# One bank of a gated product moved from VectorE to ScalarE and GpSimd in every second block

## The chip, the cores and the metric

The kernel runs on one core of a Trainium2 chip. The metric is the device time of one launch in microseconds, from the first to the last instruction, with what the launch adds around it. One core has five engines that run side by side, each working through its own instructions in order: TensorE (PE in the profile; matmul), VectorE (DVE), ScalarE (ACT), GpSimd (POOL) and SyncE (SP), which here issues DMA transfers. Matmuls write to PSUM, which has 8 banks of 512 f32 values in each of 128 partitions; here GpSimd's instructions read and write SBUF only.

## The reference, cut to what matters

The input x is 4 batches of 12416 tokens with 128 channels. Two attention stages over 32 inducing vectors come first, then a gated feed-forward layer on all 49664 tokens:

```python
h = mab(I, x)              # 32 vectors look at all tokens of a batch (stage one)
y = mab(x, h)              # all tokens look at the 32 results (stage two)
gate = 1 / (1 + exp(-(y @ w_gate)))      # 128 -> 1536
val = y @ w_val                          # 128 -> 1536
out = (gate * val) @ w_out               # 1536 -> 128
```

`mab(q, kv)` is softmax(q kv^T / sqrt(128)) kv.

## The kernel before, in words

The result of stage two is never formed. Its softmax weights (32 per token) are multiplied with h w_gate and h w_val, which are small, so a hidden matmul has only 32 rows to contract. The gate is computed as 0.5 (1 + tanh(z / 2)); the 0.5 is applied at the end.

**Blocks and slots.** The tokens are worked in 97 *blocks*: 96 of 512 tokens (24 for each batch) and one of the four left-over chunks. The 1536 hidden units of a block are 12 chunks of 128 (j = 0 to 11). They are taken in *steps* that alternate between two chunks (two PSUM banks) and one chunk (one bank): 8 steps a block. Two steps are a *slot*: four slots a block, 388 in all, 96 a batch. Slots are counted from 0, within the kernel or, where said, within a batch.

**One step** has these parts. `product(t)` (L713) does the hidden matmuls of v (`hidden_mm`, L688) and then VectorE's product u = (t + 1) v (L717), which reads tanh's output t from SBUF and v from PSUM. `gate(t+2)` (L706) does the hidden matmuls of g and ScalarE's tanh (L711) two steps ahead. Each of v's and g's two-bank and one-bank tiles exists once, so v of step t + 2 can start when the product of step t has been read out, and g of step t + 2 when the tanh of step t has. Together with the output accumulator (`acc`) and one bank for side work (`m`) that is all eight banks.

**Projection.** After each odd step `project` (L725) takes chunks from a list in the order of j, up to three in a usual slot, and adds u times w_out into `acc`, four matmuls a chunk (L733). Behind the last chunk of a block ScalarE scales the block's output (L745) and SyncE stores it. That happens in the first slot of the next block.

**Side work** is what prepares later blocks: stage two of a group of 16 chunks (four blocks), stage one of the next batch, and the combining of stage one's sums. These are Python generators. `beside(slot)` (L819) runs once a slot, after the even step's product and gate: it starts what is due, issues DMA loads of x (from GpSimd) and transposes (from SyncE), and advances every active generator by one piece (`advance`, L794). A bare `yield` ends the slot's piece; "take" and "give" hold and free bank `m`, one holder at a time. All order is fixed when the program is written, and each engine then runs its instructions in that order, as soon as their inputs are there. The pieces that matter below:

- `stage2` (L468), 20 slots ahead of its group: scores on TensorE in two halves, VectorE's maximum and GpSimd's split of it into "hi" and "lo" (L371), their two matmuls onto the scores and ScalarE's exp (L384), the sums on GpSimd (L398), GpSimd's inverse by pow (L424), the normalised weights spread four times (`s2_spread`, L447, 128x2048 on GpSimd), and a transposing DMA from SyncE (L457). The last "group" of a batch is a single chunk.
- `stage1` (L248): scores and VectorE's maximum, ScalarE's exp with its sum, a transpose by DMA, six slots later 16 matmuls and a ScalarE copy.
- `combine` (L303): small copies on GpSimd (quad, L310), four VectorE minima, ScalarE's weights w1 (L322), GpSimd's products and an adding tree over the seven groups' sums (L325 to L333, called the tree below), then matmuls that give h and h w of the next batch.

Of the kernel before, what the change touches and what calls it, by code (L numbers as in the profile page):

```python
# [9 lines left out]
F32 = mybir.dt.float32  # L10
F16 = mybir.dt.float16
BF16 = mybir.dt.bfloat16
AF = mybir.ActivationFunctionType
ALU = mybir.AluOpType
AX = mybir.AxisListType

P = 128
GC = 16
# [9 lines left out]
def kernel(  # L28
# [9 lines left out]
    nc = tc.nc  # L38
    B, N, C = x.shape
    m = inducing.shape[0]  # L40
    F = moe_w_gate.shape[1]
    NJ = F // P
# [14 lines left out]
    bp = ctx.enter_context(tc.tile_pool(name="bp", bufs=2))  # L57
    s1p = ctx.enter_context(tc.tile_pool(name="s1p", bufs=4))
    s2p = ctx.enter_context(tc.tile_pool(name="s2p", bufs=2))
    up = ctx.enter_context(tc.tile_pool(name="up", bufs=6))  # L60
    tp = ctx.enter_context(tc.tile_pool(name="tp", bufs=4))
    op = ctx.enter_context(tc.tile_pool(name="op", bufs=4))

# [23 lines left out]
    def x_transpose_dma(b, s):  # L89
# [16 lines left out]
        out=identf[:],  # L106
        in_=identf[:],
# [140 lines left out]
    def stage1(b, s):  # L248
        yield "take"
        s1 = s1_score(b, s, "m")  # L250
        yield
        yield
        a1T = s1_exp(b, s, s1)
        yield "give"
        yield
        if groups[s][1] == GC:
            a1 = s1_turn_dma(b, s, a1T)
            for _ in range(S1_LAG):
                yield
            yield "take"  # L260
        else:
            yield "take"
            a1 = s1_turn_copy(s, s1_turn_pe(b, s, a1T))
            yield
        s1_sum(b, s, a1, "m")
        yield "give"


    hT16 = {}
# [33 lines left out]
    def combine(b):  # L303
        q = b % 2
        nm1, l1, hst = nm1s[q], l1s[q], hsts[q]
        while summed[b] < NS:
            yield
        quad = bp.tile([m, 4, NS], F32, tag="quad")
        for g in range(4):
            nc.gpsimd.tensor_copy(out=quad[:, g, :], in_=nm1[32 * g : 32 * g + 32, :])  # L310
        for _ in range(COMBINE_LAG):
            yield
        col = bp.tile([P, 1], F32, tag="col")
        for g in range(4):
            nc.vector.tensor_reduce(
                out=col[32 * g : 32 * g + 32, :],
                in_=quad[:].rearrange("k g s -> k (g s)"),
                axis=AX.X,
                op=ALU.min,
            )  # L320
        w1 = bp.tile([P, NS], F32, tag="w1")
        nc.scalar.activation(out=w1[:], in_=nm1[:], func=AF.Exp, bias=col[:], scale=-1.0)  # L322
        yield
        lw = bp.tile([P, NS], F32, tag="lw")
        nc.gpsimd.tensor_tensor(out=lw[:], in0=l1[:], in1=w1[:], op=ALU.mult)  # L325
        add_tree(lw, NS)
        e32l = bp.tile([P, m], F32, tag="e32l")
        nc.gpsimd.tensor_scalar_mul(out=e32l[:], in0=e32[:], scalar1=lw[:, 0:1])
        hx = bp.tile([P, NS, C], F32, tag="hx", bufs=1)
        nc.gpsimd.tensor_tensor(  # L330
            out=hx[:], in0=hst[:], in1=w1[:].unsqueeze(2).to_broadcast((P, NS, C)), op=ALU.mult
        )
        add_tree(hx, NS)  # L333
        for _ in range(COMBINE_LAG):
            yield
        yield "take"
        l_ps = ps.tile([P, m], F32, tag="m", name="l_ps")
        nc.tensor.matmul(l_ps[:], ones[:], e32l[:], start=True, stop=True)
        li = l_inverse(l_ps[:])
        yield "give"  # L340
        yield "take"
        h_ps = ps.tile([P, m], F32, tag="m", name="h_ps")
        nc.tensor.matmul(h_ps[:], hx[:, 0, :], e32[:], start=True, stop=True)
        h_take(b, h_ps[:], li)
        yield "give"
        yield


        hwt = bp.tile([P, NI, P], F16, tag="hw", bufs=B)
        for hf in range(2):  # L350
            yield "take"
            hw_ps = hw_fill(b, hf, "m")
            nc.scalar.copy(out=hwt[:, ts(hf, NI // 2), :], in_=hw_ps[:])
            yield "give"
        hw[b] = hwt
# [88 lines left out]
        )  # L444
        return rs[:, 0:n]

    def s2_spread(n, e, rs, eng):  # L447
        a2n = s2p.tile([P, GC, 4, m], F16, tag="a2n")
        eng.tensor_tensor(  # L449
            out=a2n[:, 0:n, :, :],  # L450
            in0=e.unsqueeze(2).to_broadcast((P, n, 4, m)),
            in1=rs.unsqueeze(2).unsqueeze(3).to_broadcast((P, n, 4, m)),
            op=ALU.mult,
        )
        return a2n
# [10 lines left out]
            a2[(b, c + j)] = (a2r, j)  # L466

    def stage2(b, c, n, soon=False):  # L468
        yield "take"
        s2 = ps.tile([P, GC, m], F32, tag="m", name="s2_ps")  # L470
        half = (n + 1) // 2
        s2_score(b, c, 0, half, s2)
        yield
        s2_score(b, c, half, n, s2)
        hi, lo = s2_max(n, s2)
        yield
        yield
        e = s2_exp(n, s2, hi, lo)
        yield "give"
        sme = s2_sum_pool(n, e)  # L480
        yield
        yield
        rs = (s2_inverse if soon else s2_inverse_pool)(n, sme)
        a2n = s2_spread(n, e[:, 0:n, :], rs, nc.gpsimd)
        yield
        yield
        s2_turn_dma(b, c, n, a2n, "a2r" if n == GC else "a2l")
# [15 lines left out]
    for p in range(-2, NS - 3):  # L503
# [11 lines left out]
        if p + 1 == EARLY - 1:  # L515
# [3 lines left out]
                out=nml[:, 0:1], in_=nm1[:, 0:EARLY], axis=AX.X, op=ALU.min  # L519
# [27 lines left out]
    c0, n = groups[sc]  # L547
# [17 lines left out]
    for g in range(4):  # L565
        nc.gpsimd.tensor_copy(out=quad[:, g : g + 1], in_=ml[32 * g : 32 * g + 32, :])
    nc.gpsimd.tensor_scalar(
        out=quad[:, 0:1],
# [105 lines left out]
    steps = []  # L674
# [6 lines left out]
    blocks.append([(b, 0, NLO) for b in range(B)])  # L681
    for i in range(len(blocks)):
        for j in range(0, NJ, 3):
            steps.append(dict(block=i, j0=j, cnt=2))
            steps.append(dict(block=i, j0=j + 2, cnt=1))
    NST = len(steps)

    def hidden_mm(st, what):  # L688
# [24 lines left out]
    def product(t):  # L713
        st = steps[t]
        hidden_mm(st, "v")
        st["u"] = up.tile([P, st["cnt"], 512], F16, tag=f"u{st['cnt']}", name="u16")
        nc.vector.scalar_tensor_tensor(  # L717
            out=st["u"][:], in0=st["t"][:], scalar=1.0, in1=st["v"][:], op0=ALU.add, op1=ALU.mult
        )

    acc = [None]
    queue = [(t, k) for t in range(NST) for k in range(steps[t]["cnt"])]
    queue.reverse()

    def project(upto, now, room):  # L725
        while queue and queue[-1][0] < upto and room > 0:
            t, k = queue.pop()
            st = steps[t]
            j = st["j0"] + k
            if j == 0:  # L730
                acc[0] = ps.tile([P, BC, C], F32, tag="acc", name="acc_ps")
            for i in range(BC):
                nc.tensor.matmul(  # L733
                    acc[0][:, i, :],
                    st["u"][:, k, ts(i, P)],
                    wo16[:, j, :],
                    start=(j == 0 and i == 0),
                    stop=(j == NJ - 1),
                    skip_group_check=True,
                )  # L740
            room -= 1
            if j == NJ - 1:
                block = blocks[st["block"]]
                o32 = op.tile([P, BC, C], F32, tag="o32")
                nc.scalar.mul(out=o32[:], in_=acc[0][:], mul=0.5)  # L745
                if len(block) == 1:
                    b, c, nb = block[0]
                    nc.sync.dma_start(ov[b, :, c : c + nb, :], o32[:])
                else:
                    nc.sync.dma_start(ov0[:, 0, :, :], o32[:])  # L750
                if now < NST:
                    return
# [38 lines left out]
    def taken():  # L791
        return holder[0] is not None or slot_now[0] < free_at[0]

    def advance(gen):  # L794

        if gen["ask"]:
            if taken():
                return
            holder[0] = gen
            gen["ask"] = False  # L800
        while True:
            try:
                said = next(gen["it"])
            except StopIteration:
                active.remove(gen)
                return
            if said == "take":
                if taken():
                    gen["ask"] = True
                    return  # L810
                holder[0] = gen
            elif said == "give":
                holder[0] = None
                free_at[0] = slot_now[0] + 1
                return
            else:
                return

    def beside(slot):  # L819
        slot_now[0] = slot  # L820
        while loads and loads[0][0] <= slot:
            _, what, b, g = loads.pop(0)
            if what == "x":
                x_load(b, g)
            else:
                x_transpose_dma(b, g)
        while work and work[0][0] <= slot:
            _, first, make = work.pop(0)
            active.append(dict(it=make(), ask=False, first=first))
        for gen in sorted(active, key=lambda e: e["first"]):  # L830
            advance(gen)

# [48 lines left out]
```

## Time and profile before

| | |
|---|---|
| median of 3 runs | 768.11 us (766.72 to 768.52) |
| the profiled execution's own time | 768.34 us |
| its span, first to last instruction | 766.5 us |
| mean granted TensorE clock | 0.989 |
| L717, VectorE's products, two banks | 388, mean 1220 ns |
| L717, VectorE's products, one bank | 388, mean 679 ns |
| L711, tanh, two banks and one bank | 388 each, mean 1030 and 606 ns |
| L745, block outputs on ScalarE | 97, mean 606 ns |
| L449, spread on GpSimd, 128x2048 | 23, mean 3610 ns |
| L427, pow of the inverse on GpSimd, 128x16 | 22, mean 2936 ns |

A line of the timeline gives the start in us, the time until the merged instructions end, the engine, the line of the kernel, the operation, output and inputs, and how many instructions are merged; in brackets stands how long the engine idled before and who released it. Instructions of one engine overlap a little (the next one starts before the last has written its end), so the distance between two starts is less than a duration; where that distance matters it is taken from the starts. A hidden step's time from start to start of the two-bank products is called the slot's length.

### The profile page before, as it was taken

Reading aid. Unit: us, or ns where it says so; the run is one execution under the profiler, and the core shown is the slowest. Engines: PE = TensorE matmul, PEld = TensorE weight load, DVE = VectorE, ACT = ScalarE, POOL = GpSimd, SP = SyncE. Lnnn points to the kernel's source line nnn. Section 1 sums busy time; section 2 is a strip of 40 time slices with the busy share of each in tenths; the row PEclk is TensorE's granted clock in tenths of the full one; section 3 lists DMA queues with packets and bytes.
Section 4 is the critical chain, followed back from the end, with each engine's and each line's share of the span. In section 5 each row is a group of like instructions: output and inputs, shape, how many; then the busy total and the mean of one; then the engine's idle time right before and its main releaser. Section 6 shows DMA issues by size and latency. Waiting matters only on the chain.

```text
span 766.5 us, 20798 instructions
## 1 busy us (share of the span) xinstructions
PE 669.1 (87%) x8167; PEld 402.6 (53%) x8167; DVE 736.3 (96%) x911; ACT 672.4 (88%) x1008; POOL 275.7 (36%) x439
## 2 busy tenths in 40 slices
PE   6788889889888888989888888888998888888887
PEld 4445555555555455555555545555555555555554
DVE  4889999999999999999999999999999999999997
ACT  4689889899898989989998989989999989889896
POOL 3535050582350441545513504147335135135100
PEclk9689999999999999999999999999999999999999
DMA  8979752604249525244138342121221121231211
GB/s 168 154 144 181 149 83 84 112 29 98 71 92 178 115 63 112 57 97 86 49 78 158 88 89 63 49 57 36 78 57 49 52 68 41 58 69 34 67 43 43
DMA packets 117730, 65.16 MB, mean 85 GB/s; under 512 B 101344, under 2 KB 102016, under 8 KB 117632
## 3 DMA queue, kind: packets, MB, share of 16 engines
q1 hardware_dynamic: 112192, 49.94, 27.9%
q0 software_dynamic: 5440, 13.90, 11.1%
q8 instruction: 64, 1.05, 0.6%
q14 instruction: 34, 0.28, 0.1%
HBM read 27.80 MB, written 25.43 MB: 69 GB/s over the span
## 4 chain that ended last, share of the span: by engine, by line
DVE 34%; PE 28%; issue 20%; ACT 14%; POOL 4%; DMA 1%; ACTq 0%; DVEq 0%; POOLq 0%
DVE u L717 30%; PE acc_ps L733 11%; PE v_ps L696 11%; ACT t L711 10%; PE s_ps L362 2%; DVE nm L190 2%; DVE nmx L373 2%; ACT a1T L203 1%; PE g_ps L696 1%; ACT e L395 1%; ACT o L745 1%; PE xt_ps L494 1%; POOL near L427 1%; PE s_ps L386 1%; DMA xn<-in_x_dram 1%
## 5 line engine op out<-in xcount | busy, mean ns | idle before, releaser
L717 DVE SCALAR_TENSOR_TENSOR u<-t,v_ps 128x1024 f16<-128x1024 f16 (+1 forms) x776 | 692.2, 950 | 11.3 <-ACT t L711 3.4
L711 ACT ACTIVATE t<-g_ps 128x1024 f16<-128x1024 f32 (+1 forms) x776 | 598.2, 818 | 68.2 <-PE g_ps L696 53.8
L696 PE MATMUL v_ps<-a2r,hwt 32*128 32x512 f16 (+1 forms) x1188 | 292.8, 371 | 79.3 <-DVE u L717 76.3
L733 PE MATMUL acc_ps<-wo,u 128*128 128x128 f16 x4656 | 328.6, 220 | 1.1
L733 PEld LDWEIGHTS <-u 128*128 128x128 f16 x4656 | 262.7, 98 | 97.4 <-issue 95.6
L696 PE MATMUL g_ps<-a2r,hwt 32*128 32x512 f16 (+1 forms) x1188 | 296.1, 378 | 0.3
L696 PEld LDWEIGHTS <-hwt 32*128 32x128 f16 x2400 | 100.0, 91 | 214.6 <-issue 168.7
L377 POOL CAST hi<-nmx 128x16 bf16<-128x16 f32 (+2 forms) x28 | 5.5, 196 | 320.4 <-DVE nmx L373 288.1
L449 POOL TENSOR_TENSOR a2n<-e,rs 128x2048 f16<-128x2048 f16 (+2 forms) x28 | 86.9, 3105 | 8.3 <-DVE rs L421 3.5
L427 POOL TENSOR_TENSOR near<-sme,minus 128x16 f32<-128x16 f32 (+1 forms) x26 | 66.9, 2572 | 1.9
L745 ACT ACTIVATE o<-acc_ps 128x512 f32<-128x512 f32 x97 | 58.8, 606 | 4.1 <-PE acc_ps L733 4.1
L403 POOL TENSOR_TENSOR sum<-e 128x256 f32<-128x256 f16 (+1 forms) x27 | 16.2, 599 | 72.2 <-ACT e L395 72.2
L403 POOL TENSOR_TENSOR sum<-sum 128x128 f32<-128x128 f32 (+3 forms) x108 | 31.5, 292 | 8.5
L362 PEld LDWEIGHTS <-xT 128*128 128x128 f16 x388 | 13.6, 97 | 12.5 <-issue 12.4
L362 PE MATMUL s_ps<-hT,xT 128*128 128x32 f16 x388 | 18.2, 179 | 0.7 <-DVE hT L288 0.5
L373 DVE TENSOR_REDUCE nmx<-s_ps 128x16 f32<-128x512 f32 (+2 forms) x28 | 17.0, 607 | 0.0
L203 ACT ACTIVATE a1T<-s_ps,nm 128x512 f16<-128x512 f32 (+1 forms) x24 | 15.0, 627 | 1.7 <-DVE nm L190 1.7
L190 DVE TENSOR_REDUCE nm<-s_ps 128x1 f32<-128x512 f32 (+1 forms) x24 | 14.8, 615 | 0.9 <-PE s_ps L178 0.9
L83 POOL DMA_DIRECT2D xn<-in_x_dram x25 | 15.1, 613 | 1.1 <-POOLq L865 0.8
L395 ACT ACTIVATE e<-s_ps 128x512 f16<-128x512 f32 (+2 forms) x28 | 14.9, 533 | 0.6 <-PE s_ps L386 0.6
L498 ACT COPY xT<-xt_ps 128x1024 f16<-128x1024 f16 (+1 forms) x6 | 5.6, 940 | 8.1 <-PE xt_ps L494 8.1
L496 DVE COPY xT<-xt_ps 128x1024 f16<-128x1024 f16 (+2 forms) x8 | 4.7, 598 | 8.3 <-PE xt_ps L494 8.3
(105 smaller groups left out, 200.0 us busy)
## 6 DMA issues: line engine op xcount, KB each, us to landing
out_dram<-o SPq DMA_DIRECT2D x97, 256.0 KB, 2.4
xn<-in_x_dram POOLq DMA_DIRECT2D x19, 512.0 KB, 6.6
xn<-in_x_dram POOLq DMA_DIRECT2D x4, 544.0 KB, 6.3
a2r<-a2n SPq DMA_TRANSPOSE x29, 5.1
xn<-in_x_dram POOLq DMA_DIRECT2D x1, 384.0 KB, 13.9
wg<-in_moe_w_gate_dram POOLq DMA_DIRECT2D x1, 384.0 KB, 4.5
wv<-in_moe_w_val_dram POOLq DMA_DIRECT2D x1, 384.0 KB, 5.8
wo<-in_moe_w_out_dram POOLq DMA_DIRECT2D x1, 384.0 KB, 5.4
```

The lines of the kernel that those rows point to most:

```text
L190: nc.vector.tensor_reduce(out=nm[0:R, col], in_=s1[0:R, 0 : w * P], axis=AX.X, op=ALU.max, negate=True)
L203: nc.scalar.activation(out=a1T[0:R, 0 : w * P], in_=s1[0:R, 0 : w * P], func=AF.Exp, bias=nm[0:R, col], accum_out=l1[0:R, col],)
L362: nc.tensor.matmul(s2[:, j, :], xT[b][:, c + j, :], hT16[b][:], start=(j == 0), stop=whole and j == j1 - 1, skip_group_check=True,)
L373: nc.vector.tensor_reduce(out=nmx[:, 0:n], in_=s2[:, 0:n, :], axis=AX.X, op=ALU.max, negate=True)
L403: nc.gpsimd.tensor_tensor(out=d[:, 0:n, :], in0=src[:, :, 0:w], in1=src[:, :, w : 2 * w], op=ALU.add)
L427: nc.gpsimd.tensor_tensor(out=near[:, 0:n], in0=sme[:, 0:n], in1=minus1[:, 0:n], op=ALU.pow)
L449: eng.tensor_tensor(out=a2n[:, 0:n, :, :], in0=e.unsqueeze(2).to_broadcast((P, n, 4, m)), in1=rs.unsqueeze(2).unsqueeze(3).to_broadcast((P ...
L696: nc.tensor.matmul(pt[:, k, col : col + nb * P], hw[b][r : r + 32, j // 2, :], a2r[r : r + 32, o : o + nb, :].rearrange("p j t -> p (j t)" ...
L711: nc.scalar.activation(out=st["t"][:], in_=st["g"][:], func=AF.Tanh, scale=0.5)
L717: nc.vector.scalar_tensor_tensor(out=st["u"][:], in0=st["t"][:], scalar=1.0, in1=st["v"][:], op0=ALU.add, op1=ALU.mult)
L733: nc.tensor.matmul(acc[0][:, i, :], st["u"][:, k, ts(i, P)], wo16[:, j, :], start=(j == 0 and i == 0), stop=(j == NJ - 1), skip_group_chec ...
L745: nc.scalar.mul(out=o32[:], in_=acc[0][:], mul=0.5)
```

## The change

In the third slot of the blocks 5, 7, ..., 95 (46 blocks, called shared) the two-bank product is split. VectorE multiplies the first bank only. ScalarE copies the second bank of v to SBUF as f32; GpSimd adds 1 to t and multiplies. The result ("far") stands in a tile of its own, and its chunk, j = 7, moves to the end of its block's projection list. The instruction that closes the block is now the one that comes last in that list.

A new word "rest" is put into the side work's generators: a generator that says it isn't advanced while the slot is the second or third of a shared block. It stands ahead of stage one's exp and of its sum, ahead of w1 and of the tree in `combine`, ahead of its last fills, and in `stage2` ahead of the exp, the inverse and the spread. The spread is done in two halves in two slots, the inverse a slot earlier than before. `stage2` also waits at its start until its batch's h is there. Buffers of u go from 6 to 5 and of the output from 4 to 3, which makes room for the new tiles.

```diff
-    up = ctx.enter_context(tc.tile_pool(name="up", bufs=6))
+    up = ctx.enter_context(tc.tile_pool(name="up", bufs=5))
...
-    op = ctx.enter_context(tc.tile_pool(name="op", bufs=4))
+    op = ctx.enter_context(tc.tile_pool(name="op", bufs=3))
+    vp = ctx.enter_context(tc.tile_pool(name="vp", bufs=1))
...
+        yield "rest"
         a1T = s1_exp(b, s, s1)
...
+        yield "rest"
         w1 = bp.tile([P, NS], F32, tag="w1")
         nc.scalar.activation(out=w1[:], in_=nm1[:], func=AF.Exp, bias=col[:], scale=-1.0)
         yield
+        yield "rest"
         lw = bp.tile([P, NS], F32, tag="lw")
...
+        while b not in hT16:
+            yield
         yield "take"
         s2 = ps.tile([P, GC, m], F32, tag="m", name="s2_ps")
...
+        yield "rest"
         e = s2_exp(n, s2, hi, lo)
         yield "give"
         sme = s2_sum_pool(n, e)
         yield
-        yield
+        yield "rest"
         rs = (s2_inverse if soon else s2_inverse_pool)(n, sme)
-        a2n = s2_spread(n, e[:, 0:n, :], rs, nc.gpsimd)
+        yield
+        yield "rest"
+        a2n = s2p.tile([P, GC, 4, m], F16, tag="a2n", name="a2n")
+        half = (n + 1) // 2
+        s2_spread(half, e[:, 0:half, :], rs[:, 0:half], nc.gpsimd, a2n[:, 0:half])
+        if half < n:
+            yield
+            yield "rest"
+            s2_spread(n - half, e[:, half:n, :], rs[:, half:], nc.gpsimd, a2n[:, half:n])
         yield
         yield
         s2_turn_dma(b, c, n, a2n, "a2r" if n == GC else "a2l")
...
-            steps.append(dict(block=i, j0=j, cnt=2))
-            steps.append(dict(block=i, j0=j + 2, cnt=1))
+            off = i % 2 == 1 and 4 <= i < len(blocks) - 1 and j == 6
+            steps.append(dict(block=i, j0=j, cnt=2, shared=off))
+            steps.append(dict(block=i, j0=j + 2, cnt=1, shared=False))
...
-        nc.vector.scalar_tensor_tensor(
-            out=st["u"][:], in0=st["t"][:], scalar=1.0, in1=st["v"][:], op0=ALU.add, op1=ALU.mult
-        )
+        k = 1 if st["shared"] else st["cnt"]
+        near = nc.vector.scalar_tensor_tensor(
+            out=st["u"][:, 0:k, :],
+            in0=st["t"][:, 0:k, :],
+            scalar=1.0,
+            in1=st["v"][:, 0:k, :],
+            op0=ALU.add,
+            op1=ALU.mult,
+        )
+        if st["shared"]:
+            vc = vp.tile([P, 512], F32, tag="vc")
+            far = nc.scalar.copy(out=vc[:], in_=st["v"][:, 1, :])
+            tc.declare_no_dep(far.ins, near.ins, reason="each reads a bank of its own")
+            t1 = vp.tile([P, 512], F32, tag="t1")
+            nc.gpsimd.tensor_scalar_add(out=t1[:], in0=st["t"][:, 1, :], scalar1=1.0)
+            st["far"] = vp.tile([P, 512], F16, tag="far", name="far", bufs=2)
+            nc.gpsimd.tensor_tensor(out=st["far"][:], in0=t1[:], in1=vc[:], op=ALU.mult)
...
-    queue = [(t, k) for t in range(NST) for k in range(steps[t]["cnt"])]
+    queue = []
+    for i in range(len(blocks)):
+        mine = [(t, k) for t in range(i * 2 * NJ // 3, (i + 1) * 2 * NJ // 3) for k in range(steps[t]["cnt"])]
+        queue += sorted(mine, key=lambda e: steps[e[0]]["shared"] and e[1] == 1)
...
+            last = not queue or steps[queue[-1][0]]["block"] != st["block"]
...
+            u = st["far"][:] if st["shared"] and k == 1 else st["u"][:, k, :]
...
-                    stop=(j == NJ - 1),
+                    stop=last,
...
-            if j == NJ - 1:
+            if last:
...
+    def quiet():
+        return slot_now[0] % 4 in (1, 2) and steps[8 * (slot_now[0] // 4) + 4]["shared"]
...
+        if gen["rest"]:
+            if quiet():
+                return
+            gen["rest"] = False
...
+            if said == "rest":
+                if quiet():
+                    gen["rest"] = True
+                    return
```

## The prediction

> **What bounds the kernel now.** I read the page first (busy shares, the chain that ended last), then one undisturbed slot in the timeline, then the slots that are longer, then GpSimd's queue.
>
> ```profile
> PE 669.1 (87%) x8167; PEld 402.6 (53%) x8167; DVE 736.3 (96%) x911; ACT 672.4 (88%) x1008; POOL 275.7 (36%) x439
> ...
> DVE 34%; PE 28%; issue 20%; ACT 14%; POOL 4%; DMA 1%; ACTq 0%; DVEq 0%; POOLq 0%
> ```
>
> VectorE is busy 96% of the span, yet the chain that ended last is only 34% VectorE; TensorE and "issue" hold 48%. So VectorE is full but takes turns with somebody. The timeline of a plain slot shows with whom (first the products, then the rest of the slot):
>
> ```profile
> 404.85 1.82 DVE L717 SCALAR_TENSOR_TENSOR u<-t,v_ps 128x1024 f16<-128x1024 f16 x2
> ...
> 405.99 1.85 DVE L717 SCALAR_TENSOR_TENSOR u<-t,v_ps 128x512 f16<-128x512 f16 x2
> ```
>
> ```profile
> 404.35 0.39 PE L696 MATMUL v_ps<-a2r,hwt 32*128 32x512 f16 x2
> ...
> 404.82 1.51 ACT L711 ACTIVATE t<-g_ps 128x1024 f16<-128x1024 f32 x2 [0.26 <-PE g_ps L696]
> ...
> 404.95 0.37 PE L696 MATMUL v_ps<-a2r,hwt 32*128 32x512 f16 x1 [0.20 <-DVE u L717]
> ...
> 405.27 0.84 PE L733 MATMUL acc_ps<-wo,u 128*128 128x128 f16 x12
> ...
> 406.12 0.39 PE L696 MATMUL v_ps<-a2r,hwt 32*128 32x512 f16 x2
> ```
>
> A product of two banks starts at 404.85 (1.22 us long by the rows of its shape), one of one bank at 405.99, the next of two at 406.62: a slot is 1.772 us, 1.14 + 0.63. The two-bank product ends at 406.07; 0.05 later (406.12) TensorE refills its banks; 0.50 after that start the next two-bank product starts. 1.22 + 0.05 + 0.50 = 1.77: the single pair of v banks makes a **ring** that is as long as VectorE's own work. Where the ring has slack (after a reduce, 413.67 to 414.27) a one-bank product paces 0.595, so VectorE's own floor is about 1.73 a slot. TensorE's side has little slack too: from the single hidden matmul (404.95) 0.32 to the output projection, 12 matmuls 0.056 apart, then the refill. In the slot of a stage-two exp TensorE is the late one:
>
> ```profile
> 397.07 0.39 PE L696 MATMUL v_ps<-a2r,hwt 32*128 32x512 f16 x2
> ...
> 397.93 0.39 PE L696 MATMUL v_ps<-a2r,hwt 32*128 32x512 f16 x1
> 398.25 0.67 PEld L733 LDWEIGHTS <-u 128*128 128x128 f16 x12 [0.23 <-issue]
> ...
> 399.03 0.39 PE L696 MATMUL v_ps<-a2r,hwt 32*128 32x512 f16 x2
> ```
>
> Here the single matmul to refill is 1.10 (397.93 to 399.03) and nothing waits in it: that is TensorE's shortest way through three chunks. In the plain slot it is 1.17. So TensorE is only 0.07 us ahead of the ring. This slot is 1.97 long, 0.195 more than a plain one.
>
> **The change, part by part.** There are 46 shared blocks (odd, 5 to 95).
>
> *The third slot.* VectorE's product loses a bank: 1.139 to 0.634, 0.505 saved, 23.2 us over 46 if all of it counted. It does not: after the shorter product v is free at 0.73 us, but TensorE still has the single matmul (0.10 after the product's start), 0.32, three chunks and 0.15 ahead of the refill, which starts at 1.20 instead of 1.27. The next two-bank product starts at 1.70, and VectorE idles some 0.4. Gain 0.075 a block. Three third slots (38, 134, 230 of 388) also hold a stage-one reduce; there VectorE has use for the time, 0.45 each.
>
> *ScalarE's copy* has the shape of the output copy (L745, 128x512 f32 from PSUM, 0.605 alone, 0.477 in a row). ScalarE works 1.38 a plain slot, so 0.39 is free and the copy fits within a slot; but it stands ahead of the next tanh (1.46 instead of 0.99 after the product's start at its end), and the gate refill behind that tanh shifts by 0.3. VectorE and ScalarE reading two banks of one tile at once is in the trace: L496 and L498 both start at 12.26.
>
> *GpSimd's add and multiply.* Rows of two inputs: 256 elements 0.67, 128 0.46, so 512 is 1.08; the add of one input I bound by 0.45 and 1.07 and take 0.7. No row shows these shapes. Either end leaves it hidden in an idle queue: the bank is wanted some 4 us after the copy.
>
> *The projection order.* The bank j=7 now goes last. By the rules of project() the fourth slot projects two chunks and the next block's first slot four. Four chunks cost TensorE 12 + 4 matmuls: 1.10 + 4 x 0.056 = 1.32 against the ring's 1.17 to 1.19: **+0.135 each**, unless a reduce lengthens the slot. Two chunks save 0.22, which pays only where TensorE is late: the exps of stage two, which stand in the fourth slot of every fourth block, lose their 0.195. But an exp there (0.477 on ScalarE), behind the copy, holds the gate refill ahead of the four chunks: 0.12 more in the slot behind it.
>
> *Rests.* I followed the planner's rules slot by slot, both ways; the reduces in the trace of before sit in the slots that this gives. Three stage-one exps (0.66 with their accumulator read, 417.01 to 417.67) move from the third to the fourth slot (23, 119, 215): they lose their own 0.22 there and, with the copy ahead and four chunks behind, cost 0.64 more than a plain one.
>
> *Sum outside the stretches below*: 43 x -0.075 - 3 x 0.37 (third slots) + 43 x 0.135 + 15 x 0.12 - 0.3 (first slots) - 15 x 0.195 (exps) + 3 x 0.42 (moved exps) = **+1.4 us**. So the change itself is near nothing, and what remains is decided elsewhere.
>
> *The stretch that decides: combining.* For batches 1 to 3 stage one's sums are combined on GpSimd just before a single-chunk stage two. Before (slots counted within 96): weights w1 in slot 60, products and tree in 61, sum in 64, inverse and spread in 66, load and the next scores' hi and lo behind. Its queue is already full:
>
> ```profile
> 342.43 0.67 POOL L403 TENSOR_TENSOR sum<-e 128x256 f32<-128x256 f16 x1
> ...
> 345.08 2.94 POOL L427 TENSOR_TENSOR near<-sme,minus 128x16 f32<-128x16 f32 x1
> ...
> 348.99 3.61 POOL L449 TENSOR_TENSOR a2n<-e,rs 128x2048 f16<-128x2048 f16 x1
> 352.54 0.65 POOL L83 DMA_DIRECT2D xn<-in_x_dram  x1
> 353.21 0.20 POOL L377 CAST hi<-nmx 128x1 bf16<-128x1 f32 x1
> ```
>
> ```profile
> 353.46 0.18 PE L386 MATMUL s_ps<-hi,identb 128*128 128x32 bf16 x1 [0.19 <-POOL hi L377]
> ```
>
> TensorE, in order, waits for "hi": any more delay in GpSimd's queue stops the refills behind it. After the change quad, delayed by rests, comes in slot 56, the reduces in 62, w1 rests to 63 and the tree to 64, *behind* that slot's sum. Before, the tree (336.90 to 342.43, 5.5 us) ran while GpSimd would have waited for the exp of slot 63; now it can't. The chain from the exp's slot, which starts at 338.56: exp done 1.55 later (as at 399.12 against 397.56), sum 2.65, tree 5.53, inverse 3.91, spread in two halves 2 x 1.9, load 0.65, hi and its wait 0.4: the hi matmul at +18.5, against 353.46 - 338.56 = 14.9. That is 3.6, less 0.2 for the two-chunk slot: 3.4 in two batches, and 3.0 in the third, which has no load. A half spread is no row of steady running: the line through 128 elements (0.40) and 2048 (3.61) gives 1.9, a row of the prologue with 1024 elements 2.31; I take 1.9, as the prologue's runs among VectorE work of two SBUF inputs. The other end adds 2.5 us in all. **+9.8 us.**
>
> *Spread halves and late turns.* The group's transposed weights leave one slot later, which has room, but for the group before the combining in slot 59 instead of 54, wanted at the end of 63. From its exp I count sum, the shared bank, inverse, halves, quad and a load: issue at 332.8, wanted at 338.0. Transposes landed 4.3 to 9.3 us after issue: 0 to 4.1 us late, in the two batches that load x beside it. I take 0, as most rows land under 5.2, and keep +4.6 for the range.
>
> Buffers (up 5, op 3) I cost at nothing: a u tile lives under two slots, an output store lands in 2.4 us of a 7.1 us block.
>
> **Sum:** +1.4 + 9.8 = +11.2 us on the profiled execution's 768.34 (span 766.5; the median of the runs is 768.11): **779.5**.
>
> **Rivals.** (1) *VectorE's share is the bound*, and its 23.2 us come off. It needs the refill to start as soon as v is free, 0.73 instead of 1.20. For it: 96%. Against: 48% of the chain on TensorE's side, and the 1.10 above. 768.3 - 23.2 = 745; it outweighs the 11.2 as soon as a third slot is under 1.46 us long (11.2 / 46 = 0.24 under 1.70). Chance 0.08. [...]
> (2) *GpSimd's queue absorbs the tree* (the order at the combining leaves hi on time): the +1.4 alone, 769.7. Against: before already waits 0.19 there. Chance 0.17.
> (3) *Late turns* on top of the forecast: about 784. Chance 0.17.
> (4) *The two reads of v take turns* after all: the copy starts 0.77 later, the tanh behind it and the next product 0.6 later: 46 x 0.6 = 28 us, over 800. Against: L496 and L498. Chance 0.03.
>
> **How the numbers follow.** Forecast 0.55 (774 to 782), and the rivals as given. About 0.3% (2.3 us) is what a measurement tells from no change. Faster: rival 1 and a little of 2, 0.09; same: most of 2, 0.15; slower 0.76. The range takes in rival 2's lower half, rival 3 and the slow end of the spread: 768 to 787.
>
> **What would show it.** Third slots at 1.70 us, with VectorE idle before the next two-bank product; first slots after them at 1.9; three slots of over 5 us (71, 167, 263) with TensorE waiting for GpSimd's hi; tanh starting 0.45 after the shared product. Wrong if third slots fall under 1.5, or if that wait stays under 1 us.

## The result and the profile after

| | before | changed |
|---|---|---|
| median, runs | 767.81 us, 4 (766.72 to 768.52) | 795.7 us, 4 (791.21 to 796.32) |
| profiled execution, its span | 768.34, 766.5 us | 791.21, 789.4 us |
| mean granted TensorE clock | 0.989 | 0.962 |

The ratio is 1.0353 (95% interval 1.0335 to 1.037). The sign was right; the size was not: +27.9 us in the medians and +22.9 in the profiled executions, where +11.2 was forecast, and the time lies above the range. The page of the changed kernel, busy line, granted clock in 40 slices, and the chain that ended last:

```profile
PE 690.9 (88%) x8167; PEld 409.1 (52%) x8167; DVE 716.1 (91%) x911; ACT 695.4 (88%) x1054; POOL 405.5 (51%) x554
...
PEclk9599999987999999979999999999699999999999
...
PE 29%; DVE 26%; issue 18%; ACT 18%; DMA 4%; POOL 4%; ACTq 0%; DVEq 0%; POOLq 0%
```

VectorE lost 20.2 us of work (736.3 to 716.1) and the time rose. TensorE has the same 8167 matmuls and 21.8 us more busy time, so some of them ran slower. In the clock line that shows as an 8 and a 7, then a 7, then a 6, in the places of the three combining stretches (the clock was at half within 159 to 187, 347 to 358 and 552 to 566 us). The 5 at the start has its like in the line of before (a 6). DMA's share of the chain went from 1% to 4%.

Comparing slot lengths one by one: in the combining stretches (slots 58 to 76 of the first three batches) the changed kernel is 21.9 us longer (8.7, 6.2, 7.0), outside them 1.3 us. A plain shared slot, from the timeline of the changed kernel (start, time to the end, engine):

```profile
425.55 0.59 ACT L748 COPY vc<-v_ps 128x512 f32<-128x512 f32 x1
425.66 0.37 PE L716 MATMUL v_ps<-a2r,hwt 32*128 32x512 f16 x1 [0.20 <-DVE u L738]
...
425.99 0.84 PE L772 MATMUL acc_ps<-wo,u 128*128 128x128 f16 x12
...
426.76 0.39 PE L716 MATMUL v_ps<-a2r,hwt 32*128 32x512 f16 x2
...
427.26 1.22 DVE L738 SCALAR_TENSOR_TENSOR u<-t,v_ps 128x1024 f16<-128x1024 f16 x1 [0.41 <-PE v_ps L716]
```

The shared product starts at 425.56, the copy at 425.55, the refill 1.20 later, the next two-bank product at 427.26: a slot of 1.70, with VectorE idle for 0.41. This is the slot of the prediction. Near the combining, GpSimd's queue has the order of the prediction too: the sum of the group (L410) first, then the tree (L336 and its additions), then the inverse (L434):

```profile
351.77 0.67 POOL L410 TENSOR_TENSOR sum<-e 128x256 f32<-128x256 f16 x1 [3.78 <-ACT e L402]
...
355.88 1.68 POOL L336 TENSOR_TENSOR hx<-hst,w 128x896 f32<-128x896 f32 x1
...
359.92 2.94 POOL L434 TENSOR_TENSOR near<-sme,minus 128x16 f32<-128x16 f32 x1
```

The waits of TensorE in the combining stretches (us in total, times, longest):

```profile
PE s_ps L393 <- POOL hi L384: 6.2, 4, 2.8
PE g_ps L716 <- DMA a2r<-a2n: 4.8, 2, 2.7
```

TensorE waits for hi in slots 71, 167 and 263 (1.61, 1.38, 2.80 us; the fourth of the view is short, some 0.4) and for late turns in slots 63 and 159 (2.09, 2.75): five pauses, together 10.6 us. The forecast had 9.8 us of pauses. What it did not have is in the windows of the changed kernel (stretch, its length, then busy time by engine, the granted clock third from the end):

```profile
340.45:343.87 3.42, 3.41 (x53) 2.35 (x52) 3.42 (x5) 3.16 (x6) 1.24 (x2) 1.00 0.44 51
343.87:347.28 3.41, 2.07 (x24) 1.04 (x21) 3.34 (x10) 2.52 (x5) 2.44 (x4) 1.00 1.07 188
347.28:350.69 3.41, 1.21 (x4) 0.23 (x4) 1.00 (x1) 0.56 (x1) 0.70 (x1) 0.50 0.55 153
350.69:354.11 3.42, 3.42 (x24) 1.66 (x24) 1.59 (x2) 2.55 (x5) 1.94 (x6) 0.50 0.00 0
354.11:357.52 3.41, 3.41 (x30) 2.29 (x28) 2.45 (x4) 2.73 (x5) 2.99 (x7) 0.50 0.20 74
357.52:360.93 3.41, 2.86 (x38) 1.79 (x36) 3.11 (x4) 2.62 (x5) 3.18 (x5) 1.00 0.03 7
```

The late turn of slot 159 ends at 349.48, but the clock stays at half until 357.52. TensorE is then busy without a break, does 24 to 30 matmuls a stretch instead of 53, and everything waits for it. So a pause could have a second price: the clock dropped behind four of the five (all but the 1.38 us of slot 167).

### The profile page after: what moved, and what is told of

It reads as the page before. It is cut to its first block, busy times and chain, and to the rows that moved or that the text cites. A ratio compares the mean times of both kernels' runs of the same rounds, so it can differ in the third digit from the quotient of the medians.

```text
span 789.4 us, 21042 instructions
## 1 busy us (share of the span) xinstructions
PE 690.9 (88%) x8167; PEld 409.1 (52%) x8167; DVE 716.1 (91%) x911; ACT 695.4 (88%) x1054; POOL 405.5 (51%) x554
## 3 DMA queue, kind: packets, MB, share of 16 engines
q0 software_dynamic: 5440, 13.90, 10.6%
q8 instruction: 64, 1.05, 0.6%
## 4 chain that ended last, share of the span: by engine, by line
PE 29%; DVE 26%; issue 18%; ACT 18%; DMA 4%; POOL 4%; ACTq 0%; DVEq 0%; POOLq 0%
DVE u L738 23%; ACT t L731 14%; PE acc_ps L772 13%; PE v_ps L716 11%; DMA a2r<-a2n 2%; DMA xn<-in_x_dram 2%; PE g_ps L716 2%; ACT o L784 2%; DVE nmx L380 2%; PE s_ps L369 2%; ACT a1T L204 1%; DVE nm L191 1%; POOL near L434 1%; POOL a2n L457 1%; PE s_ps L393 1%
## 5 line engine op out<-in xcount | busy, mean ns | idle before, releaser
L738 DVE SCALAR_TENSOR_TENSOR u<-t,v_ps 128x512 f16<-128x512 f16 (+1 forms) x776 | 671.9, 917 | 54.8 <-PE g_ps L716 28.6
L716 PE MATMUL v_ps<-a2r,hwt 32*128 32x512 f16 (+1 forms) x1188 | 296.8, 379 | 67.6 <-DVE u L738 62.7
L772 PEld LDWEIGHTS <-u 128*128 128x128 f16 x4472 | 259.4, 99 | 112.5 <-issue 110.6
L716 PE MATMUL g_ps<-a2r,hwt 32*128 32x512 f16 (+1 forms) x1188 | 299.9, 384 | 7.3 <-DMA a2r<-a2n 4.8
L751 POOL TENSOR_SCALAR t<-t 128x512 f32<-128x512 f16 x46 | 68.9, 1497 | 74.2 <-ACT t L731 74.2
L457 POOL TENSOR_TENSOR a2n<-e,rs 128x1024 f16<-128x1024 f16 (+1 forms) x51 | 90.4, 1789 | 6.2 <-PE g_ps L716 2.8
L434 POOL TENSOR_TENSOR near<-sme,minus 128x16 f32<-128x16 f32 (+1 forms) x26 | 67.0, 2575 | 1.5
L753 POOL TENSOR_TENSOR far<-t,vc 128x512 f16<-128x512 f32 x46 | 58.2, 1266 | 4.5 <-ACT vc L748 0.9
L410 POOL TENSOR_TENSOR sum<-sum 128x128 f32<-128x128 f32 (+3 forms) x108 | 31.7, 293 | 8.5
L748 ACT COPY vc<-v_ps 128x512 f32<-128x512 f32 x46 | 27.3, 594 | 6.9 <-PE g_ps L716 2.2
L410 POOL TENSOR_TENSOR sum<-e 128x256 f32<-128x256 f16 (+1 forms) x27 | 16.2, 599 | 28.8 <-ACT e L402 28.8
L772 PE MATMUL acc_ps<-wo,far 128*128 128x128 f16 x184 | 18.8, 227 | 0.0
```

The source lines that it names most:

```text
L410: nc.gpsimd.tensor_tensor(out=d[:, 0:n, :], in0=src[:, :, 0:w], in1=src[:, :, w : 2 * w], op=ALU.add)
L434: nc.gpsimd.tensor_tensor(out=near[:, 0:n], in0=sme[:, 0:n], in1=minus1[:, 0:n], op=ALU.pow)
L457: eng.tensor_tensor(out=a2n[:, 0:n, :, :], in0=e.unsqueeze(2).to_broadcast((P, n, 4, m)), in1=rs.unsqueeze(2).unsqueeze(3).to_broadcast((P ...
L716: nc.tensor.matmul(pt[:, k, col : col + nb * P], hw[b][r : r + 32, j // 2, :], a2r[r : r + 32, o : o + nb, :].rearrange("p j t -> p (j t)" ...
L738: near = nc.vector.scalar_tensor_tensor(out=st["u"][:, 0:k, :], in0=st["t"][:, 0:k, :], scalar=1.0, in1=st["v"][:, 0:k, :], op0=ALU.add, o ...
L751: nc.gpsimd.tensor_scalar_add(out=t1[:], in0=st["t"][:, 1, :], scalar1=1.0)
```

## The experiments

Theory at this point: **hi comes late because GpSimd's queue near the combining is too full, and each pause of TensorE costs its own length and then a stretch at half clock.** Rivals: the regular part of the change (copy, four-chunk slots) is dearer than worked out; only the split, or only the rests, is at fault; the long slots behind a pause come from something else than the clock. Each ratio below is taken against the kernel before, run beside it (medians 767.44 to 768.39).

**1. The combining left alone.** Blocks 11, 13, 15 and 17 of the first three batches (12 of 46) are not shared and so cause no rests.

```diff
+ near_combine = i < 3 * len(groups[:NG]) * 4 and i % 24 in (11, 13, 15, 17)
- off = i % 2 == 1 and 4 <= i < len(blocks) - 1 and j == 6
+ off = i % 2 == 1 and 4 <= i < len(blocks) - 1 and j == 6 and not near_combine
```

> The changed kernel, but the blocks 11, 13, 15 and 17 of each of the first three batches (those around the combining) are not shared, so nothing rests in them either: 34 shared blocks instead of 46. Theory (the loss sits in the stretches where GpSimd's queue is full around the combining): all long slots vanish, the ordinary shared blocks cost next to nothing each, 1 to 2 us over before, about 769. Rival (each shared block costs by itself, through bank, copy or GpSimd): 34 of 46 parts of the loss of some 25 us stay, about 786.

Measured: 770.26 us against 767.44, ratio 1.0039 (1.0027 to 1.0052). The kernel with 34 shared blocks is 2 to 3 us longer than that of before, a little more than expected; the rest of the loss is gone with the 12. Shorter third slots give 2.85 us, the fourth slots 2.67, and the first slots behind take about 7.9: the change's own balance is against it, by little. The profiled span is 1.9 us longer than that of before (768.4 against 766.5), and a drop of the clock in slots 254 and 255 without a pause (see the end) has 1.4 of them.

**2. The rests and the halved spread without the split.**

```diff
+ odd = i % 2 == 1 and 4 <= i < len(blocks) - 1 and j == 6
- off = i % 2 == 1 and 4 <= i < len(blocks) - 1 and j == 6
- steps.append(dict(block=i, j0=j, cnt=2, shared=off))
+ off = False
+ steps.append(dict(block=i, j0=j, cnt=2, shared=off, odd=odd))
...
- return slot_now[0] % 4 in (1, 2) and steps[8 * (slot_now[0] // 4) + 4]["shared"]
+ return slot_now[0] % 4 in (1, 2) and steps[8 * (slot_now[0] // 4) + 4]["odd"]
```

> The changed kernel without the split: VectorE keeps the whole product, there is no copy and no GpSimd product, the projection order is that of before; the rests in the second and third slots of the odd blocks and the halved spread stay. Theory (the rests move the combining's tree behind the sum and hold the exp ahead of the combining back): the slots 71, 167 and 263 stay long, because hi comes late, 5 to 7 us each, with TensorE at half clock behind them; the turn of the group before is on time or nearly so, since GpSimd has 2.8 us less work per shared block; 777 to 788. Rival (the split is what costs, the rests are harmless): within 2 us of before.

Measured: 787.91 us, ratio 1.026 (1.0244 to 1.0275), clock 0.968. No bank is split, and hi is late by 3.42, 3.79 and 2.75 us. No turn is late. The reordering of the side work alone makes the pauses.

**3. The split without the rests.**

```diff
- return slot_now[0] % 4 in (1, 2) and steps[8 * (slot_now[0] // 4) + 4]["shared"]
+ return False
```

> The changed kernel without any rest: all 46 blocks split as in the change. Theory (GpSimd cannot take 2.8 us more in the stretch from the last full group's sum to the single chunk, wherever it stands): hi is on time, but the shared products of blocks 13 and 15 stand behind spreads and trees, and the projection waits for them at the block's end (slots 56, 64, 152, 160, 248, 256), 785 to 796. Rival (the rests alone are at fault): 769 to 771.

Measured: 791.12 us, ratio 1.031 (1.0282 to 1.0337). hi is in time, but now TensorE waits for GpSimd's share of the product. From the waits of this kernel:

```profile
PE acc_ps L772 <- POOL far L753: 13.8, 6, 3.5
```

The six waits stand in slots 56, 64, 152, 160, 248 and 256, where the spread and the tree are ahead of the add and the multiply. So the rests do what they are for, and have the pauses of run 2 as their price: near the combining GpSimd had no room for the extra work in either order that was run.

**4. Which rest.** As run 2, but without stage one's rests (ahead of its exp and its sum).

```diff
-         yield "rest"
          a1T = s1_exp(b, s, s1)
...
-             yield "rest"
              yield "take"
...
-             yield "rest"
          s1_sum(b, s, a1, "m")
```

> The kernel that rests without the split, with the rests of stage one taken out (ahead of its exp and its sum); those of the combining, of the last fills and of stage two stay. Theory: it is stage one's rest that costs. The exp of its last group, in slot 47 instead of 45, holds the shared bank, so the exp of stage two's group comes in 51 instead of 49 and the sums, quad, the minima and w1 all come later, until the tree stands behind the sum of slot 64. Without that rest w1 stands in 60 and the tree in 63, ahead of the sum: hi on time to within a microsecond, 768.5 to 772 in place of 788. Rival (the rests of the combining itself, ahead of w1 and of the tree, put it late): still 785 or more.

Measured: 770.68 us, ratio 1.0039 (1.0027 to 1.0052), no long slot; hi is late by 0.64 and 0.65 us in slots 71 and 167. In this kernel's queue the tree (L333) is ahead of the sum (L407):

```profile
337.95 1.68 POOL L333 TENSOR_TENSOR hx<-hst,w 128x896 f32<-128x896 f32 x1
...
341.99 0.67 POOL L407 TENSOR_TENSOR sum<-e 128x256 f32<-128x256 f16 x1
```

So with stage one's rests its last sums are held back, the combining starts later, and its tree falls behind the sum of slot 64. The other rests and the two halves cost under 3 us together. Not run: the split with these rests taken out, so that which order would suit both isn't known.

**5. and 6. The dose.** The kernel before, with a few GpSimd multiplies (128x512 f32, some 1 us each, an estimate by the line through the two-input rows of before, 0.456 us with 128 elements and 0.666 with 256) put ahead of the single chunk's hi, four in one kernel (`range(4)`) and two in the other (`range(2)`).

```diff
+ if n == NLO:
+     for _ in range(4):
+         nc.gpsimd.tensor_tensor(out=pad[:], in0=pad[:], in1=pad[:], op=ALU.mult)
  hi = s2p.tile([P, GC], BF16, tag="hi")
```

> The kernel before with four extra GpSimd multiplies of 128x512 f32 ahead of the single chunk's hi, about 4.3 us of GpSimd work, four times in the kernel (three of them behind a combining; the fourth meets an idle GpSimd). Nothing else is changed. Theory with the clock (a pause of TensorE of some 4 us costs itself and then some 3 us more, as TensorE runs at half its clock for about 8 us afterwards): 4.2 + 4.2 + 3.8 for the pauses and about 9 for the clock, together +21 us, 789. Rival without the clock (the pause costs its own length): +12 us, 780.

> As the kernel with four extra multiplies, but with two, about 2.15 us of GpSimd work. TensorE then pauses some 2.2 us in two batches and 1.7 in the third. [...]

Measured: 791.62 us with four (ratio 1.0307, 1.0291 to 1.0323) and 781.82 with two (1.0187, 1.0174 to 1.02). Nothing of the change is in these kernels. With four, the pauses are 4.59, 3.15, 3.88 and, in slot 359 where none was expected, 1.67, together 13.3 us, and the profiled span grew by 26.9. With two, they are 2.36, 2.34 and 1.64, together 6.3 us, and the profiled span grew by 13.8. The clock dropped behind all three (at 175.38, 359.70 and 547.43 us), as it had in the changed kernel at its pauses of 2.09 and 1.61 us (at 159.55 and 176.61 us). The length of the pauses alone would have given 767.44 + 6.3 = 773.7.

**7. One late turn taken out.** The change, with block 13 of the first three batches left whole (`and i not in (13, 37, 61)`), so that the group before the combining gets its weights in time.

> The changed kernel with block 13 of the first three batches left unshared (43 shared blocks). Theory: the add and the multiply of that block's shared product (1.50 + 1.27 us) and the wait of the multiply for its copy stand in GpSimd's queue between the sum and the inverse of the last full group, and put its turn late; without them the turn is on time and slots 63 and 159 fall from 4.3 and 6.1 us to about 1.8. But the pauses for hi in 71, 167 and 263 lie further on and stay, with the clock's drop, and get no shorter, or longer by what the late turn had hidden: 784 to 791. Rival (the late turn comes from the rests or the halved spread): slots 63 and 159 stay long.

Measured: 790.6 us, ratio 1.0298 (1.0284 to 1.0312). Slots 63 and 159 are back at 1.77, and hi is late by 3.45, 3.44 and 2.78 in slots 71, 167 and 263. A late turn had only hidden a part of the wait for hi, since it held TensorE up while GpSimd went on.

**8. What paces the regular slot.** The kernel of run 1, and in the shared blocks chunk j = 5 is left out of the projection (so it computes less).

```diff
+ if steps[8 * i + 4]["shared"]:
+     mine.remove((8 * i + 3, 0))
```

> The kernel with 34 shared blocks away from the combining, with one output chunk (j = 5) of each shared block left out of the projection, so that its output lacks that part: the third slot then projects two chunks instead of three. Theory (TensorE's three chunks ahead of the refill end VectorE's wait in a shared third slot): third slots fall from 1.70 to about 1.48 us, that is by 4 matmuls of 0.056; in all 764 to 768. Rival (ScalarE's copy ahead of the next tanh, or the refill's own latency, ends it): third slots stay at 1.70.

Measured: 766.16 us, ratio 0.9981 (0.9972 to 0.999). Plain third slots fall from 1.70 and 1.73 to 1.51 and 1.53 (1.48 was expected): with a chunk less ahead of the refill VectorE's next product starts 0.2 earlier. TensorE's three chunks end VectorE's wait there, as the prediction had it.

**9. to 11. The clock by itself.** In the kernel with two GpSimd multiplies, TensorE gets eight or four matmuls of zero columns ahead of the three hi matmuls, on columns of the score bank that nobody reads. TensorE just idles less, and hi comes no earlier: with eight, the first hi matmul starts at 174.53 us instead of 174.01. The third kernel is run 7 with 15 such matmuls; the diff is that with eight.

```diff
  def s2_exp(n, s2, hi, lo):
+     if n == NLO:
+         singles[0] += 1
+         if singles[0] <= 3:
+             for _ in range(8):
+                 nc.tensor.matmul(
+                     s2[:, 1:GC, :],
+                     identb[:],
+                     warm[:].rearrange("p (c k) -> p c k", k=m),
+                     start=False,
+                     stop=False,
+                     skip_group_check=True,
+                 )
```

> This is the run with two GpSimd multiplies ahead of the single chunk's hi (781.82 us against 767.6, pauses of TensorE of 2.36, 2.34 and 1.64 us, together 6.3), and with eight more matmuls of 480 zero columns (some 0.18 us each, 1.5 us together) that TensorE does in front of the three hi matmuls, on columns of the score bank that nobody reads. hi comes no earlier for it. Theory (the part of the cost that goes beyond the pauses comes from the clock that drops after an idle TensorE): the idle part shrinks to some 0.9, 0.9 and 0.2 us, the clock stays at 1.00 behind it, the slots behind 71, 167 and 263 keep their lengths of before, and the time is 767.7 + 6.3 = 774 us (773 to 775). Rival (the excess follows from the late hi itself: late sums, a late turn, a ring that has to be refilled): the extra matmuls change nothing that matters, 781 to 783 us.

> The same with four such matmuls (0.7 us): idle stretches of some 1.6, 1.6 and 0.9 us are left. The shortest that dropped the clock so far was 1.61, the longest that did not 1.38. If one unbroken idle stretch of about 1.6 us is what counts, the first two lie on the edge: 774 us if the clock holds in all three, up to 780 if it drops in the first two. If what counts is the busy share over a longer window, the drop comes in the same places as without the four and the time stays at 780 to 782.

> This is the change with block 13 of three batches left whole (790.6 us: the turns are in time, hi is late by 3.45, 3.44 and 2.78 us of idle TensorE), with 15 matmuls of zero columns (2.7 us) ahead of the three hi matmuls. Theory: the clock stays at 1.00, slots 71, 167 and 263 stay at 5.5 to 6.2 us, and the 11.2 us that the slots behind them had grown by come off: 779 to 781 us, which is the forecast's own sum (+1.4, and hi late by 9.7 us in all). Rival (the slots behind are long for another reason than the clock): 788 to 792 us.

Measured: 774.98 us with eight (ratio 1.0087, 1.0066 to 1.0108), 776.79 with four (1.0111, 1.0093 to 1.0129), 777.81 for run 7 with 15 (1.0125, 1.0106 to 1.0143; it was 790.6 without). The same pause of GpSimd, in the windows of the kernel with two multiplies and no extra matmuls:

```profile
171.97:175.38 3.41, 1.27 (x16) 0.86 (x15) 1.49 (x2) 1.50 (x3) 2.55 (x7) 1.00 0.95 140
175.38:178.79 3.41, 3.41 (x28) 2.05 (x27) 2.11 (x4) 1.79 (x4) 2.36 (x9) 0.50 1.01 244
178.79:182.21 3.42, 3.42 (x28) 1.52 (x22) 2.36 (x3) 2.57 (x4) 0.00 (x0) 0.50 0.26 86
```

and of the kernel with eight:

```profile
172.39:175.81 3.42, 2.72 (x23) 1.42 (x22) 1.54 (x2) 1.55 (x3) 2.62 (x6) 1.00 0.89 129
175.81:179.22 3.41, 3.11 (x39) 1.89 (x37) 2.99 (x5) 2.89 (x5) 2.37 (x9) 1.00 1.04 255
```

TensorE is busy for 2.72 us of the first stretch instead of 1.27, the clock stays at 1.00, and the slots behind 71, 167 and 263 have their lengths of before (1.84, 1.83 and 1.83, where they had 3.05 in all three). Work that computes nothing takes 6.8 us off one kernel and 12.8 us off the other. The excess over the pauses is the clock. With four matmuls, pauses of 1.43 and 1.44 us are left in slots 71 and 167; the clock dropped behind both, for two stretches and for one, and held in slot 263, so that the time lies between the 774 and the 780 that were forecast for that run. The kernel with 15 is a little faster than the 779 to 781 expected: slots 71, 167 and 263, which were to stay at 5.5 to 6.2 us, went down to 5.37, 5.38 and 4.72 as well.

## Why the prediction was wrong, point by point

**The regular part** was right: third slots 1.70 (1.73 behind a reduce), first slots behind them 1.92 (forecast 1.9), 2.06 after an exp, the moved exps +0.71 to +0.77 (forecast 0.64), exps in fourth slots 1.77. Tanh starts 0.47 after the shared product (forecast 0.45) in plain slots, and 0.82 after it in slots behind a reduce. Sum forecast +1.4 (the terms as printed add up to 1.3), traced 1.3; the errors of single terms went both ways, so that a sum this close is in part luck.

**Combining, +9.8**: the order in GpSimd's queue and the delay were right, *in pauses of TensorE*. With the late turns out (run 7) hi is late by 3.45 + 3.44 + 2.78 = 9.7 us. **The failed step is that a pause was priced at its own length**; the sum has no term for the clock. From 100 us on, the profiled execution of the changed kernel has 41 us at half clock, which is 12 stretches of 3.41 us, and that of before has none. What a stretch costs comes from the dose runs: (13.8 - 6.3) / 7 stretches = 1.07 us with two multiplies; (26.9 - 13.3) / 13 = 1.05 with four. Twelve cost some 12.7 us. The books for the profiled execution: +1.4, pauses 10.6, clock 12.7, less some 2 that I had not counted (with the minima moved, slot 60 has 1.77 instead of 2.50 in each batch) = +22.7, measured +22.9. The clock's term is an estimate by a mean price from other kernels, so that this close a fit is in part luck. Run 11 is the check: with the clock held and the turns in time the change costs +9.4 us in the medians, where the forecast without late turns was +11.2.

**Late turns, taken at 0**: wrong in the two batches named, those that load x beside it. In the second, the turn was issued at 341.13, wanted at 346.73, and landed at 349.44, 8.3 us after its issue, within the 4.3 to 9.3 quoted. From issue to want it had 5.6 us (forecast 5.2), so the term that failed is the landing, taken as that of most rows. The trace of before has the row for this very turn: issued at 143.34, 324.74 and 506.01, it took 6.8, 7.7 and 4.3 us in the three batches, and 332.8 + 7.7 is 2.5 past the 338.0. The rival that was to add 4.6 us in such a case (a figure that the prediction doesn't work out) came true in the waits (2.09 + 2.75 = 4.8), but hi then waited less: the pauses together are 10.6 and not 9.8 + 4.8.

**GpSimd's rows.** The groups of the changed kernel (count | busy, mean ns):

```profile
L751 POOL TENSOR_SCALAR t<-t 128x512 f32<-128x512 f16 x46 | 68.9, 1497 | 74.2 <-ACT t L731 74.2
L753 POOL TENSOR_TENSOR far<-t,vc 128x512 f16<-128x512 f32 x46 | 58.2, 1266 | 4.5 <-ACT vc L748 0.9
```

The add takes 1.50 us, above both of my bounds (0.45 and 1.07), the multiply 1.27 instead of 1.08; half a spread takes 1.91 (taken 1.9). Rows of before warned of it: operations on one tensor and a scalar took 0.375 us with 32 elements (L328) and 0.609 with 128 (L530), and the line through them gives some 1.5 for 512. Away from the combining that stays hidden. Near it, it is 1 us more per shared block in the queue that made the turns late; how much of their lateness is due to it wasn't tried alone.

**The rivals.** VectorE's share as the bound (745) is out: third slots are 1.70, run 8 moves the slot with a chunk of TensorE, and in run 1, where nothing comes late, less work on VectorE did not lower the time either. GpSimd absorbing the tree (769.7) is out for the change, but holds once stage one's rests are gone (run 4, 770.68, without the split) or the combining is left alone (run 1, 770.26). Reads that take turns are out: in a plain shared slot copy and product start together (425.55 and 425.56), and one-bank products keep their mean of 679 ns.

**Still open**: the median of the changed kernel lies 4.5 us above its profiled execution. Only that one has a trace; two of the three others show a mean clock of 0.957 and 0.958 against its 0.962, which would be about two more stretches at half clock (0.0045 x 795 x 2 / 3.41), some 2 us; the third shows 0.963 and is 3.9 us above all the same, so the clock explains less than half.

## What to carry to other kernels

A pause of TensorE was not paid for by its length alone here (with two multiplies, 6.3 us of pauses cost 13.8 of the span): look up in the trace what the clock does behind pauses of that size, and put its price into the sum. Moving work to an engine that is 36% busy says nothing of the stretch in which its queue is full; find that stretch first, and count what stands ahead of the instruction that others wait for. If such a wait can't be avoided, matmuls on zeros in front of it kept the clock at 1.00 here: eight of them in each of three places, which filled some 1.8 us of the pause of 2.36 in the first, were worth 6.8.

## What the runs showed of the hardware

**The clock dropped for whole stretches of 3.41 us, on a grid.** In the changed kernel all four drops begin and all end at the same phase of a 3.413 us grid (159.55 to 166.37, 176.61 to 186.85, 347.28 to 357.52, 552.08 to 565.73): the last two begin 204.80 us apart, which is 60 x 3.413. In most other kernels the grid has another phase. What nearly always told a drop was how busy TensorE had been in the stretch before it. Followed stretch by stretch from 100 us on, the kernels here have 33 drops: 31 come behind a stretch with at most 2.34 us of 3.41 busy, and of the stretches that kept the clock only two had clearly less (2.15 and 2.30, both in run 2). The two other drops came behind 2.45 us (run 3) and 2.72 us (run 8), more than many stretches that kept it, so the busy share alone is not the whole rule; what else counts stays open. Nearly all other stretches have 2.41 and more, so that these kernels ran near the edge throughout. It fits that the 1.38 us pause of slot 167 cost no clock: the grid cut it in two, and its stretches were busy for 2.47 and 2.58 us. The stretch need not be idle throughout: one that was idle for less than a third (2.34 of 3.41 us busy, run 9) had a drop behind it. Behind stretches of 2.20 us busy and more, the half clock lasted one stretch; behind emptier ones it lasted two to five, but for two in run 3 (0.94 and 0.57 us busy), where it lasted one.

**It also happened without a long pause.** In the kernel with eight matmuls on zeros, slots 158 and 159, whose schedule is that of before, lost 1.43 us together. Its windows there:

```profile
336.54:339.95 3.41, 2.33 (x24) 1.36 (x24) 3.41 (x5) 3.36 (x6) 0.82 (x5) 1.00 0.20 77
339.95:343.36 3.41, 3.41 (x23) 1.51 (x21) 2.56 (x4) 2.30 (x5) 3.15 (x5) 0.50 0.00 0
343.36:346.78 3.42, 2.84 (x38) 1.70 (x36) 2.84 (x4) 2.73 (x5) 3.03 (x7) 1.00 0.00 0
```

TensorE waits there for VectorE twice (0.66 and 0.44 us) while the combining's minima run; in the profiled execution of before the same slots keep the clock. Slots 254 and 255 have such a drop in runs 1, 4, 9 and 10 and none in the others. Whether it depends on how the grid happens to fall in an execution isn't shown: each program has one trace.
